# Scores in steps of four PSUM banks with shared diagonal columns, and earlier weight loads, in a planned two-layer attention and feed-forward kernel

## Chip, cores and metric

The kernel runs on one core of one Trainium2 chip. The metric is device time in microseconds (us) of one launch; a run's number is the median of several launches.

## The reference, cut to what matters

Input `x` is 2048 tokens by 512 numbers in bf16. Two kinds of layer alternate, with the same weights each time: attention, feed-forward, attention, feed-forward.

```
x = x + A(layernorm(x)); x = x + B(layernorm(x)); x = x + A(layernorm(x)); x = x + B(layernorm(x))

A: q, k, v = x @ wq, x @ wk, x @ wv           # 32 heads of 16; 4 segments of 512 tokens
   for each segment s:
      p = softmax(q_s k_s^T / 4 + causal mask)          # within the segment
      o_s = g * (phi(q_s) M) / (phi(q_s) z + 1e-6) + (1 - g) * (p v_s)      # g = sigmoid(beta), per head
      M += phi(k_s)^T v_s;  z += sum of phi(k_s)        # phi(t) = t + 1 where t > 0, else exp(t)
   return o @ wo                                         # 512 x 512
B: (gelu(x @ w_gate) * (x @ w_up)) @ w_down             # 512 x 1792, 512 x 1792, 1792 x 512
```

## The kernel before, in words

**Units of work.** There are eight attention blocks `Att(k)`, k = 0 to 7 (four segments, two layers), and eight feed-forward blocks `Ffn(k)`. Everything is kept in SBUF; activations stay transposed (features on partitions). A dense product `product` (L458 to L463) is four matmuls side by side in the four 32-column strips of the array, over 512 moving columns; `dense` strings four or fourteen of them into one PSUM bank, and `evict` (L454 on VectorE, L455 on ScalarE, whichever the plan finds free first) or an addition (L1054, into the residual) empties it.

**Scores.** `steps_of(k)` cuts the causal score blocks of a segment into 20 steps. The heads come in chunks `b` of eight: four groups of 32 partitions, each with an even head in the first 16 rows and an odd one in the last 16 (`par` 0 and 1). A step fills four banks of 512 columns, one per group, with matmuls in the four 32-row strips of the array (L893): for even heads `kf` with 16 rows is the stationary side, for odd heads `kB`, a copy of the keys in which the even rows are zero. `scores` then issues the exp (L924) in two halves of two banks, 128 x 1024 each, into `pt`, and GpSimd masks the diagonal blocks of 128 x 128 (`affine_select`, L911). The score banks `st0` and `st1` (two each) are fixed, and four banks `m0` to `m3` serve all else.

```
sts = {n: psp.tile([P, 2, L], F32, tag=f"st{n}", bufs=1, name="st") for n in halves}
...
if all(free):
    return (0, 1)
other = any(not j[4] and j[0] <= st_free[1] for j in ck.act.jobs)
return (0,) if free[0] and (idle and k >= HALF_FROM or k < HALF_STEPS and not other) else ()
```

So a step may be visited in two halves (`score_now`): the first as soon as its two banks are free, the second later. `flush_item` (L957) multiplies the masked exps with the values `vaug` (four strips of columns again, with the row sum as a 17th value), and VectorE transposes, divides and transposes back (L981 to L996). For `k` in `SPLIT`, which is the last block only, queries go in two halves of 256, so that the feed-forward behind it can start on the first half (`self.parts` = 2).

**The order of work** is a plan made while the kernel is built. `Clocks` and `Engine` model every engine's time with costs written in the code. A loop at the end picks for TensorE, at the modelled time, a score step if its inputs are there and its banks free, else the next operation of the open item, else the ready item with the smallest due time (`DUE`, `DUE_STEP`, `BIAS`). If nothing is ready and scores are still to come, it issues one product on the constant tile `warm` as filler (L1347, printed at L463). Other engines take jobs by ready time plus a slack. The result is a fixed order on each engine; on the chip, semaphores enforce the data's order.

**Loads** go on SP's queue. `x`, key, query and value weights come first (L333 to L340); the others are `pieces` with planned times: third input segment at 14 us, fourth at 27, output projection 32, gate 37, up 49.8, down 94. The same queue issues the DMA transposes of normed rows (`turn_later`, L428), of phi(k) and of the memory's part, and the shift of the odd heads' keys into `kB` (L636).

**The start** is written out by hand (L1183 to L1249): 19 warm-up products (`WARM`, L366), the norms of the first four tiles, transposes on TensorE, the first key and query columns, and one first score step at a planned 9.9 us.

## Time and profile before

| | |
|---|---|
| median of 3 runs | 557.91 us (557.37 to 557.98) |
| profiled execution's span, first to last instruction | 555.8 us |
| TensorE busy | 547.5 us, 99% |
| VectorE / ScalarE / GpSimd busy | 434.5 / 447.8 / 233.3 us |
| exps of scores, L924 | 320 of 128 x 1024, 1026 ns each |
| masks, L911 | 414, 204.4 us |
| filler on `warm`, L463 | 80 matmuls |

The profiled execution's own time outside the profiler is not given apart from its span; the median of the runs lies 2.1 us above the span. PE is TensorE's matmuls, PEld its weight loads, DVE VectorE, ACT ScalarE, POOL GpSimd, SP the queue that issues most DMAs. In a row of a group stand the line, the engine, the operation, out<-in, shapes and count, then the busy time and the mean of one in ns, then the idle time just before and what ended it. In a row of stretches stand the stretch, its length, and the busy time (and instructions) of PE, PEld, DVE, ACT and POOL, then TensorE's granted clock, the DMA share and GB/s.

### The profile page before, as it was taken

The numbers are of one execution on the slowest core, as the hardware profiler recorded it, in microseconds if no ns is written. First come the engines' busy times: TensorE is split into PE (matmuls) and PEld (weight loads), VectorE is DVE, ScalarE is ACT, GpSimd is POOL, SyncE is SP. The second block draws the span as 40 slices with busy tenths as digits, with TensorE's granted clock in tenths as the row PEclk, the third lists the DMA queues.
The fourth block names the chain that finished last, engine by engine and source line by source line (L and its number), as shares of the span: only waits on it lengthen the run. The fifth ranks groups of instructions, "written<-read, shape, count | busy, mean of one in ns | idle before, by whom it ended". The sixth has DMA issues, their size and how long they took to land.

```text
span 555.8 us, 25686 instructions
## 1 busy us (share of the span) xinstructions
PE 547.5 (99%) x11557; PEld 272.5 (49%) x11557; DVE 434.5 (78%) x820; ACT 447.8 (81%) x544; POOL 233.3 (42%) x470
## 2 busy tenths in 40 slices
PE   8999999999999999999999999999999999999997
PEld 4433344444454444444444444544454444545996
DVE  5978797999969898687967889489876898587161
ACT  5899999987998878987898978988889877973500
POOL 5675664255624455144632555155632562021000
PEclk9999999999999999999999999999999999999999
DMA  7248710610152024220230205101320104020001
GB/s 228 40 107 220 150 25 13 168 37 2 22 60 50 12 31 69 40 41 2 41 50 12 42 2 86 33 16 28 79 59 3 22 13 87 3 22 31 14 4 40
DMA packets 65261, 27.87 MB, mean 50 GB/s; under 512 B 54720, under 2 KB 64704, under 8 KB 65152
## 3 DMA queue, kind: packets, MB, share of 16 engines
q1 hardware_dynamic: 65008, 26.23, 23.3%
q8 instruction: 90, 1.47, 1.1%
q14 instruction: 19, 0.16, 0.1%
q10 hardware_dynamic: 144, 0.01, 0.0%
HBM read 9.71 MB, written 2.10 MB: 21 GB/s over the span
## 4 chain that ended last, share of the span: by engine, by line
PE 88%; DVE 6%; DMA 2%; POOL 1%; ACT 1%; issue 1%; SPq 0%; ACTq 0%
PE m L463 71%; PE st L893 9%; PE m L957 6%; DVE xn L522 2%; PE m L366 1%; ACT pt L924 1%; DVE byq L981 1%; DVE x_sb L1054 1%; DMA xnT<-xn 1%; DMA amT<-am 1%; POOL rs L509 1%; POOL pt L911 1%; DVE st L486 0%; DVE ab L989 0%; DVE xnT L454 0%
## 5 line engine op out<-in xcount | busy, mean ns | idle before, releaser
L924 ACT ACTIVATE pt<-st 128x1024 bf16<-128x1024 f32 x320 | 309.8, 1026 | 55.5 <-PE st L893 49.8
L911 POOL TENSOR_SCALAR_AFFINE_SELECT pt<-pt 128x256 bf16<-128x256 bf16 (+2 forms) x414 | 204.4, 510 | 265.5 <-ACT pt L924 249.5
L463 PE MATMUL m<-wd_sb,gel 128*32 128x512 bf16 x1792 | 106.1, 380 | 0.4 <-DVE x_sb L1054 0.4
L463 PE MATMUL m<-xnT,wg_sb 128*32 128x512 bf16 (+1 forms) x2016 | 105.4, 356 | 0.8 <-DVE byq L981 0.5
L463 PE MATMUL m<-xnT,wu_sb 128*32 128x512 bf16 (+1 forms) x2016 | 106.0, 356 | 0.1
L1141 DVE TENSOR_TENSOR gel<-gel,m 128x512 bf16<-128x512 bf16 x112 | 75.3, 682 | 34.3 <-PE m L463 31.6
L463 PEld LDWEIGHTS <-wu_sb 128*32 128x32 bf16 x2016 | 52.3, 97 | 40.0 <-issue 4.8
L463 PEld LDWEIGHTS <-wg_sb 128*32 128x32 bf16 x2016 | 51.7, 97 | 39.7 <-issue 5.9
L463 PEld LDWEIGHTS <-gel 128*32 128x32 bf16 x1792 | 50.6, 97 | 40.3 <-issue 5.0
L1054 DVE TENSOR_TENSOR x_sb<-x_sb,m 128x512 bf16<-128x512 bf16 x64 | 42.2, 671 | 22.5 <-PE m L463 22.4
L981 DVE STREAM_TRANSPOSE byq<-m 128x512 f32<-128x512 f32 x64 | 45.2, 706 | 11.5 <-PE m L957 11.4
L957 PE MATMUL m<-pt,vaug 128*32 128x256 bf16 (+3 forms) x1096 | 46.3, 292 | 0.0
L1106 ACT ACTIVATE gel<-m 128x512 bf16<-128x512 f32 x63 | 34.9, 602 | 11.0 <-PE m L463 11.0
L893 PE MATMUL st<-q,kB 32*128 32x256 bf16 (+3 forms) x548 | 41.0, 290 | 0.0
L486 DVE BATCH_NORM_STATS2 st<-x_sb 128x6 f32<-128x512 bf16 x60 | 40.6, 677 | 0.3
L893 PE MATMUL st<-q,kf 16*128 16x256 bf16 (+3 forms) x548 | 39.1, 293 | 0.5 <-ACT q L1228 0.5
L463 PE MATMUL m<-xnT,wq_sb 128*32 128x512 bf16 (+1 forms) x528 | 36.5, 374 | 0.7 <-DVE xnT L564 0.5
L463 PE MATMUL m<-xnT,wk_sb 128*32 128x512 bf16 (+2 forms) x528 | 35.9, 374 | 0.0
L893 PEld LDWEIGHTS <-kf 16*128 16x128 bf16 x548 | 12.2, 91 | 45.5 <-issue 44.3
L957 PEld LDWEIGHTS <-vaug 128*32 128x32 bf16 x1096 | 24.3, 96 | 20.7 <-issue 7.8
L522 DVE TENSOR_SCALAR xn<-x_sb,mv,rs 128x512 bf16<-128x512 bf16 x64 | 29.9, 512 | 2.8 <-POOL rs L509 2.6
L463 PE MATMUL m<-wv_sb,xnT 128*32 128x512 bf16 x512 | 32.1, 380 | 0.0
(91 smaller groups left out, 539.7 us busy)
## 6 DMA issues: line engine op xcount, KB each, us to landing
out_dram<-x_sb SPq DMA_DIRECT2D x16, 128.0 KB, 2.2
wg_sb<-in_B_w_gate_dram SPq DMA_DIRECT2D x8, 224.0 KB, 3.5
kB<-kf SPq DMA_DIRECT2D x28, 64.0 KB, 2.5
wu_sb<-in_B_w_up_dram SPq DMA_DIRECT2D x8, 224.0 KB, 3.9
wd_sb<-in_B_w_down_dram SPq DMA_DIRECT2D x7, 256.0 KB, 3.1
x_sb<-in_A_x_dram SPq DMA_DIRECT2D x3, 512.0 KB, 6.3
xnT<-xn SPq DMA_TRANSPOSE x48, 3.2
x_sb<-in_A_x_dram SPq DMA_DIRECT2D x4, 128.0 KB, 2.8
```

What stands on the lines that cost most here:

```text
L366: nc.tensor.matmul(ps[:], lhsT=warm[:], rhs=wide, start=True, stop=True)
L463: nc.tensor.matmul(out[r], lhsT=lhsT[:, r], rhs=rhs, start=start, stop=stop, tile_position=(0, 32 * c))
L486: nc.vector.bn_stats(out=self.st6[:, 0, :], in_=x_sb[:, self.tt0 + j, :])
L522: nc.vector.tensor_scalar(out=xn[:], in0=x_sb[:, self.tt0 + j, :], scalar1=self.mv[:, j, 0:1], scalar2=self.rs[:, j, :], op0=ALU.subtract, ...
L893: nc.tensor.matmul(sts[j // 2][:, j % 2, c0:c0 + q1 - q0], lhsT=lhsT[rows, b, P * ki:P * ki + P], rhs=self.q[rows, b, q0:q1], start=True, ...
L911: nc.gpsimd.affine_select(out=dv, in_=dv, pattern=[[0, w], [1, P]], compare_op=ALU.is_ge, fill=0.0, base=0, channel_multiplier=-1)
L924: 1.024, lambda st=st, tile2=tile2: nc.scalar.activation(out=tile2[:], in_=st[:], func=ACT.Exp, scale=SCALE), told), table="exp")
L957: nc.tensor.matmul(ps()[32 * j:32 * j + 32, q0 + shift:q1 + shift], lhsT=self.vaug[:, ki, h * (DH + 1):h * (DH + 1) + 32], rhs=step["pt"][ ...
L981: nc.vector.transpose(out=self.byq[:, c], in_=ps()[:])
L1054: ck.dve.post(ck.made(), slack, (0.683, lambda: nc.vector.tensor_tensor(out=xt, in0=xt, in1=ps()[:], op=ALU.add), lambda t: (ps.read(t), t ...
L1106: return lambda: nc.scalar.activation(out=out(), in_=in_(), func=ACT.Gelu_apprx_tanh)
L1141: ck.dve.post(ck.made(), NORMAL, (0.683, lambda: nc.vector.tensor_tensor(out=hidden(g, h), in0=hidden(g, h), in1=banked(ps), op=ALU.mult), ...
```

## The change

It does the following.

1. *Shared diagonal columns.* In a diagonal block of 128 queries, the first 64 queries see only 64 keys. `kS` holds the first 64 keys of every tile for an even and an odd head, interleaved, and one block of 64 columns gives the scores of both (`u` = 2 in the code below). Matching values `vS` are made by two DMAs per block. The other 64 queries keep their 128 keys. Steps become 18 in a segment, 19 in the first.
2. *Steps of four banks.* All eight banks are one pool. A step takes four banks, side by side if they are free, and then has one exp of 128 x 2048; otherwise two pairs. Half visits are gone. `may_open` limits how many banks other items hold.
3. *First segment by halves*: `SPLIT = {0, NK - 1}`.
4. *Port and landings in the plan*: the model of VectorE and GpSimd has jobs marked `Port` that exclude each other, and items of the first feed-forward block wait in the plan until their weights are modelled as landed.
5. *Loads*: output projection and gate from 8.8 us, third input segment 9.3, up 26, down 43.1 (three pieces) and 47 (four), fourth input segment 59.6.
6. Two sets of values and of `kB` in place of three, the masks of the memory's block in bf16, the gate folded into the division; a shorter hand-written start with 14 warm-up products; the last down product in 384 and 128 columns; and new numbers for the plan, with a table `CHANGES` that alters slacks and due times every 8 us of planned time.

The core of the diff:

```diff
-WARM = 19
-STEPS = 20
+WARM = 14
+WG_GAP, WU_GAP, WD2 = 1.1751, 1.964, 47.0
-WO, WG, X2, WU, X3, WD = 32.0, 37.0, 14.0, 49.8, 27.0, 94.0
+WO, WG, X2, WU, X3, WD = 8.92, 8.8357, 9.3414, 26.0, 59.6, 43.1
-SPLIT = {NK - 1}
+SPLIT = {0, NK - 1}
...
+    def shared(blocks, tiles):
+        return [(b, 2, t, P * t, P * t + Q, Q * (len(blocks) * m + n)) for n, b in enumerate(blocks)
+                for m, t in enumerate(tiles)]
...
+    def long(b, par):
+        return [(b, par, 3, L - Q, L, 0), (b, par, 0, Q, L, Q)], []
+    def short(b, par, ends):
+        return [(b, par, 1, P + Q, L, 0), (b, par, 2, HALF + Q, L, 320)], ends
...
+        found += [long(b, 0), short(b, 0, []), (shared((b, b + 1), range(TPS)), [(b, 0, None)]),
+                  long(b, 1), short(b, 1, [(b, 1, None)])]
+        for par in range(2):
+            found += [long(b + 1, par), short(b + 1, par, [(b + 1, par, None)])]
...
+            if isinstance(cost, Port):
+                t = next((end for who, begun, end in self.port[-24:] if who is not self and begun <= t < end), t)
+                self.port.append((self, t, t + cost))
...
     for h in range(7):
-        pieces.append((WD + 2.0 * h, 256, lambda r=r: load(
+        pieces.append(("down", (WD if h < 3 else WD2) + 0.1 * h, 256, lambda r=r: load(
...
+    big = psp.tile([P, 8, L], F32, tag="big", bufs=1, name="big")
...
+            def shared_keys(blocks, t):
+                def copy(b, u, eng):
+                    eng.tensor_scalar(
+                        out=kS[:, b, :, :, u], in0=self.kf[:, b, :].rearrange("p (t h c) -> p t h c", h=2, c=Q)[:, :, 0, :],
+                        scalar1=(maskA, maskB)[u][:, 0:1], scalar2=None, op0=ALU.mult)
+                ...
+                    for u in range(2):
+                        ck.pool.post(t, tn.KS_SLACK + 0.01 * b, (Port(1.05), lambda b=b, u=u: copy(b, u, nc.gpsimd), (
+                            lambda t2, b=b: ev.update({("kS", k, b): t2})) if u else None))
...
+    def may_open():
+        return held("m") < (tn.CAP if step_ready() else tn.CAP_FREE) and len(free_banks()) > 0
...
+    def four_banks():
+        free = free_banks()
+        for first in (4, 0, 3, 2, 1):
+            if WHOLE and all(first + i in free for i in range(4)):
+                return [first + i for i in range(4)]
+        ...
+        return [*pairs[1], *pairs[0]] if len(pairs) > 1 else None
...
+        for b, u, ki, q0, q1, c0 in parts:
+            for j in range(4):
+                rows = slice(32 * j, 32 * j + (32 if u else 16))
+                if u == 2:
+                    lhsT = kS[rows, b, ki].rearrange("p c u -> p (c u)")
+                else:
+                    lhsT = (a.kf, a.kB)[u][rows, b, P * ki:P * ki + P]
+                nc.tensor.matmul(big[:, got[j], c0:c0 + q1 - q0], lhsT=lhsT, rhs=a.q[rows, b, q0:q1], start=True,
+                                 stop=True, tile_position=(32 * j, 0))
...
+            ck.act.post(max(ready, step["at"]), tn.EXP_SLACK, (
+                0.172 + 0.000832 * width * len(banks_of), lambda g=g, st=st: nc.scalar.activation(
+                    out=pt[:, g, 0:width], in_=st, func=ACT.Exp, scale=SCALE), lambda t, g=g: told(t, g, g is groups[-1])),
+                table="exp")
...
+                return [down(j, slice(0, 3 * P)), down(j, slice(3 * P, D))]
...
+    def timely():
+        last = max((f for f, o in zip(banks, owner) if o == "s"), default=0.0)
+        return last <= ck.pe + tn.AHEAD or tn.EAGER and not opened and not any(it.ready() for it in items if it.kind != "flush")
```

In a flush, `pieces` holds, for a head, the plain blocks with `vaug` and the shared blocks with `vS`, eight in a whole flush instead of four, over the same 1280 columns. After, the plan still issues filler on `warm` where nothing is ready.

869 lines of the change are left out of this document (530 added, 339 removed).

## The prediction

> **What bounds the kernel now.** I read the page's busy table and its chain first, then the cores' clock, the busy time by stretches, the groups, the waits, and last the timeline of TensorE.
>
> ```profile
> span 555.8 us, 25686 instructions
> PE 547.5 (99%) x11557; PEld 272.5 (49%) x11557; DVE 434.5 (78%) x820; ACT 447.8 (81%) x544; POOL 233.3 (42%) x470
> PE 88%; DVE 6%; DMA 2%; POOL 1%; ACT 1%; issue 1%; SPq 0%; ACTq 0%
> core 0: 555.8 us, clock 0.999
> 40.00:60.00 20.00, 20.00 (x346) 8.05 (x340) 17.32 (x36) 19.73 (x27) 11.65 (x26) 1.00 0.81 194
> 60.00:80.00 20.00, 19.56 (x372) 8.08 (x372) 16.69 (x35) 19.47 (x24) 12.77 (x27) 1.00 0.44 93
> 300.00:320.00 20.00, 20.00 (x440) 9.24 (x436) 18.27 (x35) 17.50 (x21) 9.87 (x21) 1.00 0.19 36
> 520.00:540.00 20.00, 19.87 (x744) 19.51 (x736) 9.57 (x14) 5.86 (x10) 0.00 (x0) 1.00 0.02 4
> ```
>
> TensorE (PE) is busy in 19.6 to 20.0 of every 20 us in these stretches, and 88% of the chain is its own. It runs at full clock, so only less work on PE, or work on it that was worth nothing, can shorten the kernel. Up to 80 us ScalarE (ACT) is full too (19.5 to 19.7 of 20); at 300 it is not (17.5), and at 520 it has little left to do. So the early stage has two limits, the rest has one.
>
> What PE's time is made of shows in its timeline, the columns being start, length, engine and line, operation, count:
>
> ```profile
> 305.93 1.04 PE L463 MATMUL m<-xnT,wk_sb 128*32 128x512 bf16 x16
> 306.90 0.39 PE L893 MATMUL st<-q,kB 32*128 32x512 bf16 x4
> 307.22 2.56 PE L463 MATMUL m<-xnT,wu_sb 128*32 128x512 bf16 x44
> 511.58 3.20 PE L463 MATMUL m<-wd_sb,gel 128*32 128x512 bf16 x56
> 514.60 6.29 PE L463 MATMUL m<-xnT,wg_sb 128*32 128x256 bf16 x224
> ```
>
> Fourteen dense products of four matmuls take from 511.58 to 514.60, 0.216 us each. At 305.93 four of them should be done by 306.79, but the score matmuls of L893 begin at 306.90: 0.11 us to go from the column tiling of the dense work to the row tiling of the scores. From 306.90 to the next dense matmul at 307.22 are 0.32 us, of which 0.21 are the 512 columns and 0.11 the way back. A visit of PE to the scores costs 0.43 us, half of it for switching the tiling.
>
> ```profile
> 10.11 0.29 PE L893 MATMUL st<-q,kf 16*128 16x256 bf16 x4 [0.49 <-ACT q L1228]
> 499.88 0.29 PE L893 MATMUL st<-q,kf 16*128 16x256 bf16 x4
> PEld L893 <- issue: 71.5, 173, 0.5
> 25.28 1.48 PE L463 MATMUL m<-warm 128*32 128x512 bf16 x24
> 75.69 0.39 PE L463 MATMUL m<-warm 128*32 128x512 bf16 x4
> L463 PE MATMUL m<-warm 128*32 128x512 bf16 x80 | 5.8, 382 | 0.0
> ```
>
> The timeline has 181 separate visits, the first at 10.11 and the last at 499.88 (the weight loads of L893 waited 173 times for their turn, which is the same count less the visits that waited for data). There are only 160 steps of scores; the others are steps done in two halves, each paying the full 0.43 us. And 80 matmuls on the constant tile `warm`, that is 20 products or 4.3 us, are filler that the planner put in where nothing was ready, between 25.28 and 77 us, in the stage where ACT is full.
>
> **The change part by part.** *Four-bank steps and shared diagonals.* A segment has 20 steps before. After, the first 64 queries of each diagonal block see only 64 keys, and the keys of two heads are interleaved into one block, so the diff's `steps_of` gives 18 steps for segments 1 to 7 and 19 for segment 0: 145. Each is one visit, never half. Removed are 181 - 145 = 36 visits at 0.43 us: **-15.5 us** of PE.
>
> *Smaller pieces.* Fifteen of the 145 steps have eight parts of 64 columns in place of one or two long ones, and a flush (L957) takes four more products of 64 columns, 64 times, for the same 1280 columns. The trace has no 64-column matmul; its neighbours are these.
>
> ```profile
> 464.62 0.23 PE L893 MATMUL st<-q,kf 16*128 16x128 bf16 x4
> 464.68 0.23 PE L893 MATMUL st<-q,kB 32*128 32x128 bf16 x4
> 464.96 1.70 PE L463 MATMUL m<-wd_sb,gel 128*32 128x512 bf16 x28
> 312.97 0.64 PE L463 MATMUL m<-zcols,phiq 128*32 128x8 bf16 x64
> 313.44 1.06 PE L463 MATMUL m<-wv_sb,xnT 128*32 128x512 bf16 x16
> ```
>
> A score part of 128 columns starts 0.06 us after the one before, and the visit with four of them still ends after 0.34 us (464.62 to 464.96). Sixteen products of 8 columns took 0.47 us (312.97 to 313.44), 0.029 each, which leaves 64 columns (0.027 us of streaming) hardly dearer than streaming. If 64 columns cost as little as 0.029, a step of eight parts grows by 0.02 us and a flush by 0.01: 15 x 0.02 + 64 x 0.01 = 0.9 us. If they cost 0.06 as 128 do, it is 15 x (8 x 0.06 - 0.21) + 64 x 4 x (0.06 - 0.027) = 4.1 + 8.4 = 12.5 us. They cannot be cheaper than the columns they stream. I take **+1.5 us**, near the row of 8 columns, since the distance between 128-column parts is their streaming (0.053).
>
> *One exp over four banks.*
>
> ```profile
> L924 ACT ACTIVATE pt<-st 128x1024 bf16<-128x1024 f32 x320 | 309.8, 1026 | 55.5 <-PE st L893 49.8 <-POOL pt L911 4.6
> L455 ACT ACTIVATE q<-m 128x512 bf16<-128x512 f32 x17 | 10.3, 604 | 0.8 <-PE m L463 0.5
> 60.33 7.65 ACT L924 ACTIVATE pt<-st 128x1024 bf16<-128x1024 f32 x8
> ```
>
> From 512 to 1024 columns ACT takes 0.42 us more, so 2048 should take 1.026 + 2 x 0.42 = 1.87 us. Before, a pair takes 1.94 (309.8 / 160; the eight at 60.33 take 7.65, the same). ACT's exps go from 309.8 to 145 x 1.87 = 271, or to 281 if every step is still issued as two pairs. This is off the chain after 100 us and worth nothing there by itself. In the early stage it is what the filler waited for: at 60.33 ACT runs exps without a gap while PE runs filler. With segment 0 cut into two halves (so that its first output projection and gate products become ready after 6 steps instead of 20) and the weights loaded from 8.8 us on, I count the filler as gone: **-4.3 us** (0 at worst).
>
> *VectorE and GpSimd.* The masks shrink: a step before has up to eight blocks of 128 wide columns to mask, after it two narrow ones over half the partitions. In their place come 56 copies of keys on GpSimd (POOL) at 1.05 us by the planner's own figure, 59 us.
>
> ```profile
> L911 POOL TENSOR_SCALAR_AFFINE_SELECT pt<-pt 128x256 bf16<-128x256 bf16 x332 | 146.8, 460 | 188.5 <-ACT pt L924 173.1 <-PE m L463 9.9
> L911 POOL TENSOR_SCALAR_AFFINE_SELECT pt<-pt 128x512 bf16<-128x512 bf16 x74 | 49.4, 670 | 72.5 <-ACT pt L924 72.0
> L911 POOL TENSOR_SCALAR_AFFINE_SELECT pt<-pt 128x1024 bf16<-128x1024 bf16 x8 | 8.6, 1094 | 4.4 <-ACT pt L924 4.4
> 13.12 1.80 POOL L418 MEMSET kB<- 128x2048 bf16 x1
> 13.27 1.77 DVE L644 TENSOR_SCALAR kB<-kf,maskB 128x384 bf16<-128x384 bf16 x1
> L644 DVE TENSOR_SCALAR kB<-kf,maskB 128x512 bf16<-128x512 bf16 x3 | 1.1, 387 | 0.0
> ```
>
> An unsplit segment has 16 plain steps with two masks of 256 elements (0.46 each) and two shared ones with two of 1024 (1.09): 19 us, about 155 us over all segments against 205 before. With the copies POOL stays near 235 us. But POOL holds up VectorE (DVE): the copy at 13.27 took 1.77 us beside POOL's memset, where larger ones take 0.387. DVE has 121 us without work, so I put this at 0 on PE; what it costs if it strikes an eviction that PE waits for is a rival below. [...]
>
> *Loads.*
>
> ```profile
> wg_sb<-in_B_w_gate_dram SPq DMA_DIRECT2D x8, 224.0 KB, 3.5
> wd_sb<-in_B_w_down_dram SPq DMA_DIRECT2D x7, 256.0 KB, 3.1
> ```
>
> The output projection, the gate weights and the third segment's input (512 + 8 x 224 + 512 KB, 2.8 MB) are issued from 8.8 us, the up weights from 26, the down weights at 43 to 47 instead of 94. On SP's queue the transposes of the normed rows, the key shifts and the phi transposes come behind them. Between 40 and 60 us the kernel already moves 194 GB/s with PE at 20.00 of 20, so I cost this at 0; without that cover, 1.8 MB of down weights at that rate are 9 us that a transpose issued behind them could be late, and PE would run filler: at most 9 us.
>
> *Ends.* Warm-up falls from 19 to 14 matmuls and the first scores come some 1.6 us sooner by the planner, but the dense start stays at 11.4: 0. The last down product is cut into 384 and 128 columns:
>
> ```profile
> 552.26 0.69 DVE L1054 TENSOR_TENSOR x_sb<-x_sb,m 128x512 bf16<-128x512 bf16 x1 [2.33 <-PE m L463]
> ```
>
> The last addition, 0.69 us for 512 columns, is then about 0.29 for 128: **-0.4 us**.
>
> **The sum**: 555.8 - 15.5 + 1.5 - 4.3 - 0.4 = 537.1 us of span. The median before is 557.91, 2.1 us above the profiled span, which I add: **539.2, said as 539**.
>
> **The rivals.**
>
> *A, the early stage stays bound by ACT.* For it: 60 us to 80 has ACT at 19.47. Of the 181 visits 59 lie before 80 us by the same count; if those and the filler give nothing, the gain is 15.5 x 122/181 = 10.4, and the time 557.9 - 10.4 + 1.5 - 0.4 = 548.6. Against it: ACT's own work per segment falls by 10 to 12%.
>
> *B, slower: PE stands at the visits.* Before, the first pair of banks is free after 1.03 us of exp and a visit may begin with it; after, all four stay taken for 1.87, and the visit with everything dense behind it in PE's order waits for the last of them.
>
> ```profile
> ACT pt L924 <- PE st L893: 49.8, 80, 1.8
> PE st L893 <- ACT q L1228: 0.5, 1, 0.5
> ```
>
> The gain of the sum is 15.5 + 4.3 + 0.4 - 1.5 = 18.7 us. To make the kernel slower by more than 1.1 us (0.2%), the waits must reach 19.8 us, 0.14 us at each of 145 visits; 0.25 us at each would give 539.2 + 36 = 575. For it: the order on PE is fixed by a planner's figures, and the hand-over between exps and scores is slow already (ACT waited 49.8 us in 80 gaps for scores). Against it: PE waits for ACT once, 0.5 us, in all of before, and dense work may now use the other four banks and more.
>
> *C, POOL's copies hold up DVE where PE needs a bank.* If one in three of the 56 copies puts 0.5 us on PE, that is +9: 548. [...]
>
> ```profile
> PE m L463 <- DVE byq L981: 0.8, 3, 0.5
> ```
>
> *D, better: the start tightens too.* PE's own small waits (some 3 us in all, that row the largest after the first microsecond) and the 1.6 us by which the first scores come sooner are won as well, with 1.5 for the small pieces not paid: 539.2 - 3 - 1.6 - 1.5 = 533.
>
> **How the numbers follow.** The forecast has 0.50, A 0.15, C 0.08, D 0.12, B 0.12; 0.03 is left for a change within 0.2% (1.1 us), about what a measurement of this kernel can tell from none. The range goes from just below D, 531, to the forecast with the dear end of the small pieces (539.2 + 11 = 550.2) and A, with a little over it: 553. Faster has 0.85, the same 0.03, slower 0.12.
>
> **What would show it.** Right, if the profile after has about 145 visits of 0.43 us (0.34 to 0.5 where there are eight parts), exps of 1.87 us over 2048 columns, fewer than 20 products of `warm`, PE at 99% and steps of 64 columns at 0.03 us a part. Wrong, if PE's idle time names ACT's exp or a DVE eviction for more than a few us, if filler between 10 and 80 us grows, if the shared steps take over 0.6 us, or if a load stands in front of a transpose that PE waits for.

## The result and the profile after

The changed kernel takes 557.8 us (median of 10 runs, 556.5 to 560.3); the kernel before, on the same chip, 558.0 (10 runs, 557.4 to 558.9). The ratio is 0.9999, 95% interval 0.9985 to 1.0013: no change, where 539 (531 to 553) had been forecast. The profiled execution has a span of 554.7 us, 1.1 less than before; it is the fastest of the ten (556.5 us), and four of the others ran at a mean clock of 0.994 to 0.997, so what is read from it below leaves the last 1.3 us up to the median open.

From the page of the changed kernel, the span, TensorE's busy time and the chain; then its page's row for instruction transfers, of which the kernel before had 90 with 1.47 MB:

```profile
span 554.7 us, 29909 instructions
...
PE 540.0 (97%) x13722; PEld 293.8 (53%) x13722; DVE 432.6 (78%) x830; ACT 419.6 (76%) x386; POOL 237.9 (43%) x416
...
q8 instruction: 107, 1.75, 1.3%
...
PE 80%; DVE 9%; DMA 4%; ACT 3%; issue 2%; POOL 1%; SPq 0%; ACTq 0%; DVEq 0%; POOLq 0%
```

PE is busy 7.5 us less, but no longer 99% of the span, and 20% of the chain is other things where it was 12%. There are 4,223 more instructions. PE alone has more than these: 2,165 more matmuls, each with its weight load. The waits of PE in the changed kernel (us in total, times, longest):

```profile
PE big L654 <- issue: 2.9, 4, 1.5
PE big L1117 <- issue: 1.9, 1, 1.9
PE big L654 <- DMA xnT<-xn: 1.7, 3, 0.8
PE big L1117 <- DMA vS<-vaug: 1.2, 1, 1.2
...
PE big L1421 <- ACT pt L1491: 0.5, 2, 0.3
```

4.8 us of them are "issue": nothing that the profile shows was missing. The timeline of PE at these places, and at one with filler:

```profile
58.98 0.38 PE L1117 MATMUL big<-pt,vaug 128*32 128x256 bf16 x8
61.23 0.21 PE L1117 MATMUL big<-pt,vaug 128*32 128x64 bf16 x4 [1.88 <-issue]
...
93.50 1.69 PE L654 MATMUL big<-warm 128*32 128x512 bf16 x28
95.58 1.05 PE L654 MATMUL big<-xnT,wq_sb 128*32 128x512 bf16 x16 [0.38 <-DMA xnT<-xn]
...
116.06 0.41 PE L1421 MATMUL big<-q,kS 32*128 32x64 bf16 x32
116.40 0.51 PE L654 MATMUL big<-xnT,wu_sb 128*32 128x256 bf16 x12
116.74 0.62 PE L654 MATMUL big<-zcols,phiq 128*32 128x8 bf16 x56
118.87 0.21 PE L654 MATMUL big<-zcols,phiq 128*32 128x8 bf16 x8 [1.51 <-issue]
```

PE stops in the middle of a flush (L1117) and in the middle of 64 small matmuls (`zcols`) for which the profile shows no operand missing. At 93.50 it runs seven products of filler and then still waits for the next segment's rows.

I summed the timeline of PE from each start to the next, with gaps over 0.12 us apart:

| us of PE | before | after | change |
|---|---|---|---|
| score visits (181, 145) | 59.3 | 48.1 | -11.2 |
| dense work, with the switch into each visit | 420.8 | 416.7 | -4.1 |
| flushes | 35.9 | 38.1 | +2.2 |
| filler (20, 49 products) | 5.2 | 12.1 | +6.9 |
| gaps | 3.3 | 10.4 | +7.1 |
| warm-up | 6.8 | 5.2 | -1.6 |

With +0.2 in the small products and -0.6 at the end that is the 1.1 us. So the visits gave what they should, and filler and gaps took 14.0 us back. Two windows of the same 30 us, before and then after, show where (busy us and count of PE, PEld, DVE, ACT, POOL, then clock, DMA share, GB/s):

```profile
45.00:75.00 30.00, 30.00 (x524) 12.08 (x524) 26.46 (x56) 29.24 (x38) 17.39 (x38) 1.00 0.68 152
```
```profile
45.00:75.00 30.00, 25.99 (x960) 20.68 (x952) 23.67 (x49) 24.67 (x27) 11.30 (x16) 1.00 0.55 119
```

After, PE got 960 matmuls where it had 524, and was busy 4 us less.

### The profile page after: what moved, and what is told of

Same layout as the page of the kernel before. It is cut to its first block, busy times and chain, and to the rows that moved or that the text cites. A ratio compares the mean times of both kernels' runs of the same rounds, so it can differ in the third digit from the quotient of the medians.

```text
span 554.7 us, 29909 instructions
## 1 busy us (share of the span) xinstructions
PE 540.0 (97%) x13722; PEld 293.8 (53%) x13722; DVE 432.6 (78%) x830; ACT 419.6 (76%) x386; POOL 237.9 (43%) x416
## 3 DMA queue, kind: packets, MB, share of 16 engines
q8 instruction: 107, 1.75, 1.3%
## 4 chain that ended last, share of the span: by engine, by line
PE 80%; DVE 9%; DMA 4%; ACT 3%; issue 2%; POOL 1%; SPq 0%; ACTq 0%; DVEq 0%; POOLq 0%
PE big L654 68%; PE big L1421 7%; PE big L1117 5%; ACT pt L1491 3%; DMA amT<-am 1%; DVE xn L713 1%; DVE byq L1145 1%; DVE st L677 1%; DMA xnT<-xn 1%; DVE ab L1153 1%; POOL pt L1464 1%; DMA vS<-vaug 1%; DMA x_sb<-in_A_x_dram 1%; DVE x_sb L1218 1%; DVE aT L1160 1%
## 5 line engine op out<-in xcount | busy, mean ns | idle before, releaser
L1491 ACT ACTIVATE pt<-big 128x2048 bf16<-128x2048 f32 (+1 forms) x151 | 272.8, 1810 | 68.8 <-PE big L1421 63.7
L1464 POOL TENSOR_SCALAR_AFFINE_SELECT pt<-pt 64x256 bf16<-64x256 bf16 (+4 forms) x302 | 151.9, 530 | 232.7 <-ACT pt L1491 231.4
L654 PE MATMUL big<-xnT,wu_sb 128*32 128x512 bf16 (+1 forms) x2240 | 105.6, 337 | 0.9 <-issue 0.9
L654 PE MATMUL big<-wd_sb,gel 128*32 128x512 bf16 (+2 forms) x1848 | 105.2, 373 | 0.0
L654 PE MATMUL big<-xnT,wg_sb 128*32 128x512 bf16 (+1 forms) x2240 | 104.7, 337 | 0.0
L1308 DVE TENSOR_TENSOR gel<-gel,big 128x512 bf16<-128x512 bf16 x112 | 75.0, 682 | 32.0 <-PE big L654 26.9
L654 PEld LDWEIGHTS <-gel 128*32 128x32 bf16 x1848 | 46.6, 97 | 43.3 <-issue 3.6
L1218 DVE TENSOR_TENSOR x_sb<-x_sb,big 128x512 bf16<-128x512 bf16 (+1 forms) x65 | 43.1, 668 | 25.6 <-PE big L654 25.3
L1145 DVE STREAM_TRANSPOSE byq<-big 128x512 f32<-128x512 f32 x64 | 45.2, 706 | 20.5 <-PE big L1117 20.0
L1117 PE MATMUL big<-pt,vaug 128*32 128x64 bf16 (+5 forms) x1152 | 45.0, 263 | 2.1 <-issue 1.9
L1273 ACT ACTIVATE gel<-big 128x512 bf16<-128x512 f32 x64 | 35.2, 605 | 4.5 <-PE big L654 4.3
L1117 PE MATMUL big<-pt,vS 128*32 128x64 bf16 x960 | 28.0, 193 | 1.2 <-DMA vS<-vaug 1.2
```

Source lines behind the costliest of these rows:

```text
L654: nc.tensor.matmul(out[r], lhsT=lhsT[:, r], rhs=rhs, start=start, stop=stop, tile_position=(0, 32 * c))
L1117: nc.tensor.matmul(ps()[32 * j:32 * j + 32, q0 + shift:q1 + shift], lhsT=va[:, ki, values_of(va, b, p, j)], rhs=step["pt"][:, j, c0:c0 + q ...
L1145: nc.vector.transpose(out=self.byq[:, c], in_=ps()[:])
L1218: ck.dve.post(ck.made(), slack, (0.683 - 0.00104 * (D - width), lambda: nc.vector.tensor_tensor(out=xt, in0=xt, in1=ps()[:, 0:width], op=A ...
L1273: return lambda: nc.scalar.activation(out=out(), in_=in_(), func=ACT.Gelu_apprx_tanh)
L1308: ck.dve.post(ck.made(), NORMAL, (0.683, lambda: nc.vector.tensor_tensor(out=hidden(g, h), in0=hidden(g, h), in1=banked(ps), op=ALU.mult), ...
```

## Experiments on the filler

My first theory after the result: the filler stands where PE would wait anyway, so a shorter step on PE only makes more of it. The rival is the prediction's: filler is work on PE's path, and goes when it goes.

**a_nofill**: the changed kernel without its 44 planned filler products (five more are written into its start and stay); **b_nofill**: the kernel before without its 20.

```
-                product(ps()[:], warm[:], wide)
+                ck.tiling("columns")
```

> The changed kernel with the plan as it is, but the 44 filler products on the constant tile (9.5 us of TensorE) that the plan puts in are not issued. Theory 'cover': they stand where TensorE would wait for data anyhow, mostly for VectorE in the first 45 us and around 133 us; the time falls by 0 to 2 us and idle time of the same size appears in their place. Rival 'plan too slow': the data is there earlier than the plan thinks, the filler is in the way, and the time falls by 7 to 9.5 us, to about 549.

> The kernel before without the 20 filler products that its plan puts between 25.3 and 77 us (5.2 us of TensorE by the trace); the order of everything else is unchanged. Theory 'filler stands where TensorE would wait anyway, and keeps its granted clock up': the time doesn't fall; it stays or rises by up to 4 us (557.5 to 562), and the profile shows gaps of 1 to 2.5 us at 25 to 29 us and near 63 and 76 us, with a granted clock below 1 right behind them. Rival, the prediction's own term 'filler is work on TensorE's path that goes when it goes': 5.2 us less, near 552.8.

a_nofill took 564.2 us, 1.0113 (1.0095 to 1.0132) of the kernel before; b_nofill 559.7, 1.0040 (1.0027 to 1.0053). Both are slower. For b_nofill that is what its theory said; neither forecast for a_nofill came, since its idle time appeared but the time rose by 6.4 us. Waits, timeline and windows of a_nofill:

```profile
PE big L654 <- DMA xnT<-xn: 6.2, 2, 3.5
PE big L1421 <- ACT pt L1491: 5.6, 7, 1.9
...
25.98 0.29 PE L1421 MATMUL big<-q,kf 16*128 16x128 bf16 x4 [1.93 <-ACT pt L1491]
28.63 0.40 PE L1421 MATMUL big<-q,kf 16*128 16x256 bf16 x4 [1.27 <-ACT pt L1491]
100.75 1.00 PE L654 MATMUL big<-xnT,wq_sb 128*32 128x512 bf16 x8 [3.49 <-DMA xnT<-xn]
...
25.00:30.00 5.00, 2.75 (x48) 1.28 (x51) 4.72 (x13) 3.97 (x4) 2.45 (x3) 0.57 0.74 139
30.00:35.00 5.00, 5.00 (x84) 2.16 (x80) 3.58 (x10) 3.77 (x4) 4.21 (x6) 0.74 0.43 127
100.00:105.00 5.00, 4.25 (x96) 2.08 (x100) 1.20 (x4) 1.25 (x2) 0.33 (x1) 0.66 0.31 61
```

Where the filler of 22 to 29 us was, PE now waits for the exp to give back its banks; where the filler of 93 us was, for `xnT`. Gaps rise from 10.4 to 19.4 us and all but eat the 10.3 us of filler that went. On top the granted clock (third number from the end) falls: it is 0.50 from 25.75 to 32.57 us, from 49.64 to 53.05 and from 100.84 to 104.25, of which the stretches of 5 us show parts as 0.57 to 0.74. Its mean is 0.987, and 1.3% of 562 us is 7 us. By the same sums as in the table PE's other work takes 8.0 us longer and the end 1.0: 9.0 + 8.0 + 1.0 - 10.3 makes the 7.7 us between the spans. b_nofill closes in the same way: 5.2 us of filler gone, gaps up by 2.9, and a mean clock of 0.993 (3.9 us): +1.6, the difference of the spans (557.4 against 555.8). So filler covers waits, and without it the clock fell: a mean of 0.987 in a_nofill's profile against 1.000 in the changed kernel's, 0.993 in b_nofill's against 0.999 before.

**b_nohalf**: why are there more such waits after? The kernel before, but with its steps always on all four banks (no visit of two banks while the exp of the other two runs), the order worked out anew.

```
-HALF_FROM = 0
+HALF_FROM = NK
-HALF_STEPS = 1
+HALF_STEPS = 0
```

> The kernel before with its steps always on all four banks: no visit of two banks while the exp of the other two runs. The order is worked out anew with constants that were fitted to the other one, so its later part may be worse for that reason; what is to be read is the first 45 us, up to which the order follows the exps. Theory 'a step that takes four banks at once makes exp and visit take turns, so ACT is not kept busy in the start and TensorE waits or is filled': exps of the first 45 us no longer follow each other without a gap, ACT's busy time there falls by 2 us or more, filler there rises from 2.5 us (25 to 29 us) to 4 us or more; the whole is 5 to 20 us slower. Rival 'the start is paced by VectorE and the inputs, the steps' shape doesn't matter there': ACT's exps and the filler up to 45 us are as before within 0.5 us.

575.1 us, 1.0305 (1.0283 to 1.0326), with 25.6 us of filler. As its constants belong to another order, only the start is read. ACT's timeline there: before, then b_nohalf, then the changed kernel.

```profile
25.47 7.56 ACT L924 ACTIVATE pt<-st 128x1024 bf16<-128x1024 f32 x8 [1.75 <-PE st L893]
```
```profile
27.49 1.94 ACT L924 ACTIVATE pt<-st 128x1024 bf16<-128x1024 f32 x2 [2.96 <-PE st L893]
30.01 1.94 ACT L924 ACTIVATE pt<-st 128x1024 bf16<-128x1024 f32 x2
33.01 1.94 ACT L924 ACTIVATE pt<-st 128x1024 bf16<-128x1024 f32 x2
```
```profile
24.03 1.89 ACT L1491 ACTIVATE pt<-big 128x2048 bf16<-128x2048 f32 x1
26.89 1.88 ACT L1491 ACTIVATE pt<-big 128x2048 bf16<-128x2048 f32 x1 [0.97 <-PE big L1421]
29.39 1.88 ACT L1491 ACTIVATE pt<-big 128x2048 bf16<-128x2048 f32 x1
```

Before, the exps of two banks follow each other without a break, four steps in 7.56 us, because a visit fills one pair while ACT empties the other. On four banks at once a step comes every 2.5 to 3.0 us, in b_nohalf as in the changed kernel. ACT's busy time up to 45 us falls from 36.1 to 34.0 us (32.6 in the changed kernel), filler up to 45 us rises from 11 products to 24 (25 planned ones, and 5 in the start, in the changed kernel). The theory's numbers hold. The start is paced by exps, as the prediction saw, but it became slower in steps per microsecond although ACT had less to do: between 25 and 45 us the exps of 9 steps end before, of 6.5 in b_nohalf, of 7 in the changed kernel.

Up to 20 us, however, the exps of 3.5, 3 and 1 steps have ended. So four banks at once don't explain the changed kernel's first 20 us: there its order runs the query and key products from 11.61 to 17.9 us without a visit, where the kernel before has visits at 12.77, 13.64, 15.38 and 17.77, and ACT's second step begins at 18.67. No run tests this alone.

## Experiments that take rivals away

**a_noks**: without the 56 copies of keys on GpSimd, so later segments' diagonal columns use old keys (rival C). **a_wd60**: down weights sent for at 60 and 64 us; **b_wd61**: in the kernel before, at 62.6, the second part of the change alone. **a_2exp**: each exp of four banks as two of two.

```
-                        ck.pool.post(t, tn.KS_SLACK + 0.01 * b, (Port(1.05), lambda b=b, u=u: copy(b, u, nc.gpsimd), (
+                        ck.pool.post(t, tn.KS_SLACK + 0.01 * b, (Port(1.05), lambda b=b, u=u: None, (
...
-WG_GAP, WU_GAP, WD2 = 1.1751, 1.964, 47.0
+WG_GAP, WU_GAP, WD2 = 1.1751, 1.964, 64.0
-WO, WG, X2, WU, X3, WD = 8.92, 8.8357, 9.3414, 26.0, 59.6, 43.1
+WO, WG, X2, WU, X3, WD = 8.92, 8.8357, 9.3414, 26.0, 59.6, 60.0
...
-WO, WG, X2, WU, X3, WD = 32.0, 37.0, 14.0, 49.8, 27.0, 94.0
+WO, WG, X2, WU, X3, WD = 32.0, 37.0, 14.0, 49.8, 27.0, 62.6
...
-                    out=pt[:, g, 0:width], in_=st, func=ACT.Exp, scale=SCALE), ...
+                    out=pt[:, slice(g.start + h, g.start + h + 2), 0:width], in_=st[:, h:h + 2, :], func=ACT.Exp, scale=SCALE)
+                    for h in range(0, g.stop - g.start, 2)], ...
```

> The changed kernel without the 56 copies of keys on GpSimd (segments 1 to 7 score their shared columns against old keys; 58 us of GpSimd work left out). Theory 'port': these copies hold up VectorE where TensorE needs it; VectorE's busy time falls by 5 us or more and the time by 3 to 9 us. Rival 'off the path': the time falls by less than 1 us.

> The changed kernel with the down weights issued at 60 and 64 us of the plan instead of 43.1 and 47. The order on all engines but SP's queue stays the same. Theory 'loads': the down weights right behind the up weights hold up transposes, key shifts or the instruction stream between 43 and 72 us; then the idle time of TensorE at 46 and between 59 and 72 us (4 us) goes, and the time falls by 2 to 4 us. Rival 'not the loads': the idle time stays and the time is the same within 0.7 us.

> One part of the change alone: the kernel before, with its down weights sent for at 62.6 us instead of 94 (right behind the up weights), the order of all engines but SP's the same. Theory 'where the down weights load costs and gains nothing': 0.998 to 1.002 of the kernel before. Rival 'earlier down weights delay the segment inputs behind them (the third and later xn loads), so TensorE waits for xnT': 1 to 3 us slower, with a DMA wait near 70 to 100 us.

> The changed kernel, with each exp over four banks issued as two over two banks (1024 columns each), in the same place of the same order: 139 more ACT instructions, nothing else. In the trace of the kernel before an exp of 1024 columns took 0.94 us, in that of the changed one one of 2048 took 1.88 us, so ACT gains or loses nothing by the sums (2 x 0.94). Theory 'ACT's time is not what limits the changed kernel; TensorE's own waits are': no change, 0.998 to 1.004 of the changed kernel. Rival 'the long exp holds the four banks as one and so the first matmuls of the next visit wait the whole 1.88 us': the visit still needs all four banks in the order it writes them, so the first half would be free 0.94 us sooner; in the first 60 us, where exps follow each other every 2.6 to 2.9 us, up to 0.3 us for each of some 15 steps would come back, 3 to 5 us, ratio 0.991 to 0.995.

| run | us | ratio to before | interval |
|---|---|---|---|
| a_noks | 557.9 | 1.0003 | 0.9982 to 1.0024 |
| a_wd60 | 559.0 | 1.0023 | 1.0002 to 1.0044 |
| b_wd61 | 557.6 | 1.0001 | 0.9987 to 1.0015 |
| a_2exp | 556.9 | 0.9986 | 0.9969 to 1.0003 |

None of them is what took the gain. In a_noks VectorE is busy 428.3 us instead of 432.6, so the copies do cost it 4 us (less than the 5 expected), but PE's issue gaps stay (waits of a_noks):

```profile
PE big L654 <- issue: 2.5, 3, 1.4
PE big L1117 <- issue: 2.1, 1, 2.1
```

Loading the down weights right behind the up weights neither helps nor hurts. Sent for later, in a_wd60, the kernel took 1.2 us more than the changed kernel, which is neither of its two forecasts; the intervals of the two overlap, so it isn't known whether this is a cost. The earlier loads of the output projection, the gate and up weights and the inputs were not tested alone. One exp or two for a step makes no difference that these runs can tell.

## Experiments on the issue gaps

Theory: PE runs out of instructions where many short ones lie together. Rival: the places themselves (banks, tiling) are to blame.

**a_thin**: gate and up of the first segment issue two of their four strips, so half of these hidden units keep old data. **b_cut**: the kernel before with gate and up of its first two segments cut into products of 256 columns. (By the trace these are 896 matmuls that became 1,792, half of the numbers in the expectation.)

```
-        for c in range(4):
+        for c in range(strips):          # 2 for gate and up of k = 0
...
+                if k < 2:                # b_cut: two products of 256 columns for one of 512
+                    return [(Clocks.MM[512], lambda kt=kt, f=f: cut(kt, f)) for f in tiles(g) for kt in range(KT)]
```

> The changed kernel in which the gate and up products of the first feed-forward block, which are cut into 256 columns there, issue two of their four column strips (the other half of those hidden units keeps old data). Each product streams the same 256 columns, so TensorE's streaming time is the same, but 896 matmuls with their weight loads fewer pass through its instruction stream. Theory 'instruction supply': the idle time put down to issue (4.8 us at 59, 64, 68, 71 and 117 us) goes or shrinks to under 2 us, and the time falls by 2 to 5 us. Rival 'loads' or any other: that idle time stays over 4 us and the time is the same within 1 us.

> The kernel before with gate and up products of the first two segments cut into two of 256 columns each: 1,792 products of 512 columns become 3,584 of 256, the same columns and flops, the same order of all else. Theory 'instructions reach TensorE's queue at a limited rate, and where many short ones lie together it runs dry': the profile of this kernel shows gaps of TensorE put down to issue of 1 to 3 us in the first 150 us, which the kernel before lacks there, more KB of instruction transfers, and more time than the added 1,792 products cost by themselves. A product of 128 columns takes 0.056 us and one of 512 0.216 us in the trace, so halving costs no more than 0.005 us each, about 0 to 9 us; the gaps would come on top. Rival 'the gaps put down to issue come from the changed order's full banks or from its visits of many small pieces': no issue gap over 0.5 us here, and the time rises by 9 us at most.

a_thin: 554.9 us, 0.9958 (0.9942 to 0.9974), with 448 matmuls fewer and the same columns streamed; its issue gaps are 0.3 us in all, from 4.8. b_cut: 561.7 us, 1.0074 (1.0053 to 1.0094); its waits name one issue gap of 0.8 us at 108 us, where the kernel before has none, less than the 1 to 3 us expected. The theory passes the first run clearly and the second barely: most of b_cut's 4 us lies in the halved products themselves.

**c_whole**: the same work in fewer instructions. Gate of the first segment's first half, up of its second half and the `zcols` products of segment 2 go out as one matmul over the whole array instead of four strips: 384 fewer (a half has 56 products, not the 64 of the expectation). **c_again** is the same kernel measured once more. **c_both** adds the exps in halves. **d_whole** does so with all gate and up products of the first segment, two memory updates and the `zcols` of segment 1 as well, 864 fewer by the trace (its expectation and the later ones say 816).

```
+    def at_once(out, lhsT, rhs, start=True, stop=True):
+        ck.tiling("columns")
+        nc.tensor.matmul(out, lhsT=lhsT, rhs=rhs, start=start, stop=stop)
...
-                         lambda kt=kt, f=f, n=n: product(ps()...
+                         lambda kt=kt, f=f, n=n: (at_once if whole else product)(ps()...
```

> The changed kernel, order and filler as they are, with three stretches of products issued as one matmul of 128x128 weights each instead of four of 128x32 side by side: gate of the first segment's first half, up of its second half (64 products of 256 columns each) and the normaliser products of segment 2 (16 of 8 columns): 144 instructions where there were 576. Nothing is left out. A product takes as long as before by its columns (0.107 us for 256), and going over to whole weights and back is dearer by two switches of about 0.1 us for each of two stretches. Theory 'the issue gaps are TensorE running out of instructions, since the changed kernel has many short ones in these stretches': the gaps put down to issue at 59.4 (1.88 us) and 117.4 (1.51 us) go or shrink below 0.3 us, those at 64 to 71 (1.4 us together) shrink in part; the kernel gains 2 to 4 us, ratio to the kernel before 0.992 to 0.997. Rival 'the gaps belong to these places whatever is issued there': they stay, and the time is unchanged or 0.5 us longer.

> The kernel of the run before in this list and the exps in two halves of two banks each together. The exps in halves alone measured 0.9986 (0.9969 to 1.0003) of the kernel before, the changed kernel 0.9999: if the two add, 0.991 to 0.996. If the exps' halves do nothing, the same as the run before within 0.1%.

> The kernel with gate of the first half, up of the second half and the normaliser products of segment 2 as whole 128x128 matmuls, carried further: all gate and up products of the first segment, both memory updates of segments 0 and 1 and the normaliser products of segments 1 and 2 as whole matmuls, 816 fewer instructions than in the changed kernel in place of 384. Nothing is left out, the order and the filler are unchanged. In the profile of the run with 384 fewer, 1.1 us of issue gaps were left, nearly all at the normaliser products of segment 1 near 66 us (0.89 and 0.18). Theory 'every gap put down to issue is missing instructions': these go too; against that stand some three more switches of about 0.1 us; 0.5 to 1.2 us less than the run with 384 fewer, ratio to the kernel before 0.990 to 0.993. Rival 'the first stretches had all that there was to gain': no less than that run, 0.992 to 0.996.

| run | us | ratio to before | interval | issue gaps, waits for xnT (us) |
|---|---|---|---|---|
| changed kernel | 557.8 | 0.9999 | 0.9985 to 1.0013 | 4.8, 1.7 |
| c_whole | 553.2 | 0.9925 | 0.9908 to 0.9943 | 1.1, 1.6 |
| c_again | 553.2 | 0.9937 | 0.9913 to 0.9961 | 1.3, 2.7 |
| c_both | 554.9 | 0.9952 | 0.9934 to 0.9970 | 0.6, 5.8 |
| d_whole | 557.4 | 0.9986 | 0.9965 to 1.0006 | none, 7.8 |

The place of the second gap in c_whole's timeline, now without one:

```profile
114.41 0.50 PE L658 MATMUL big<-xnT,wu_sb 128*128 128x256 bf16 x3
114.75 0.55 PE L658 MATMUL big<-zcols,phiq 128*128 128x8 bf16 x16
115.22 1.05 PE L654 MATMUL big<-xnT,wk_sb 128*32 128x512 bf16 x16
```

So the gaps are missing instructions: with nothing left out and the same order, they go where the count falls (from 4.8 us to 1.1), and c_whole is faster than both kernels. The traces bear it out directly, since they hold the time of each transfer of instructions, a block of 16.4 KB (1.75 MB over 107). All twenty profiles together have 39 gaps of PE that are put down to issue, and each of them ends 1.2 to 1.6 us after such a block has landed. In the changed kernel there are five, 1.3 to 1.5 us behind: the one that ends at 61.23 us follows the block of 58.33 to 59.82, the one that ends at 118.87 follows that of 116.28 to 117.57. The 13,722 matmuls over 107 blocks are 128 a block on the mean, each with its weight load. In none of the profiles do two blocks begin less than 3.3 us apart (3.41 at least in the changed kernel, 3.47 before), and 128 matmuls of 256 columns take 3.6 us (212 take 5.93). Shorter ones use a block up sooner than that: in the flush from 58.42 us 44 take 0.94 us, which makes 2.7 for 128, and of `zcols` 56 take 0.62 from 116.74, which makes 1.4.

c_both adds nothing: it is 1.7 us slower than c_whole, with 5.8 us of waits for `xnT`, which is neither of its forecasts. And d_whole, which has no issue gap left, gains nothing in time: my expectation for it failed. Another wait had come up in their place.

## Experiments on the landing of the next segment

The waits of PE in d_whole, its timeline at 49 us, and what SP's queue issues before the second such wait:

```profile
PE big L654 <- DMA xnT<-xn: 7.8, 4, 2.7
...
49.39 1.05 PE L654 MATMUL big<-xnT,wq_sb 128*32 128x512 bf16 x16 [2.73 <-DMA xnT<-xn]
...
88.76 1.40 SPq L892 DMA_DIRECT2D vS<-vaug  x2
90.25 2.57 SPq L611 DMA_TRANSPOSE amT<-am  x2
92.91 2.39 SPq L611 DMA_TRANSPOSE xnT<-xn  x1
```

The change adds two transfers per segment, `vS<-vaug`, which put the values into the order of the shared diagonal blocks. They stand in SP's queue ahead of the last transposition of the next segment's rows, for which PE waits until 96.6 us.

**d_novs**: d_whole without these copies from the second segment on, so the later diagonal columns use the first segment's values. **d_vspool**: the copies issued on GpSimd's queue. **d_wu**: the up weights' pieces sent for 1.2 us apart instead of 1.96. **a_vspool** and **c_vspool**: the changed kernel and c_whole with the copies on GpSimd's queue.

```
-            ck.sp.post(t, tn.KB_SLACK, (0.55, lambda u=u, c=c: nc.sync.dma_start(
+            ck.sp.post(t, tn.KB_SLACK, (0.55, lambda u=u, c=c: nc.gpsimd.dma_start(
                            out=vS[u:P:2, :, c], in_=self.vaug[0:Q, :, c]), ...
```

> A second time the kernel with 384 fewer instructions (gate of the first half, up of the second half, normaliser of segment 2 as whole matmuls), beside the three that follow. Its first measurement was 553.18 us, 0.9925 (0.9908 to 0.9943), the kernel with 816 fewer 0.9986 (0.9965 to 1.0006) with 7.8 us of waits for xnT in its profile where this one had 1.6. Theory 'when the issue gaps are gone, the time hangs on the landing of the next segments' xnT, which differs from run to run': its times spread over 551 to 560 like those of the other, mean ratio 0.992 to 0.998. Rival 'this one is steadily faster': 0.991 to 0.9945 again.

> The kernel with 816 fewer instructions without the copies of shared values (vS) from the second segment on: 14 of the 16 transfers of 136 KB left out, so the later segments' diagonal columns use the first segment's values. The order of everything else is unchanged. Theory 'the new vS transfers, which SP issues just ahead of the next segment's last xnT transposition, delay its landing': the waits for xnT near 94 and 147 us (2.55 and 2.16 us) go or shrink below 0.8; the one at 46.7 us (2.7 us), which has no vS transfer just before it, stays; the time falls by 3 to 6 us, clock losses behind the gaps included, to 0.988 to 0.993 of the kernel before. Rival 'the transpositions themselves are late, whatever stands beside them': all three waits stay, the time within 0.2% of 0.9986.

> The kernel with 816 fewer instructions with the vS copies issued on GpSimd's queue in place of SP's: nothing is left out. In the trace SP is held 0.7 us by each of the two and 1.2 to 1.3 by each transposition behind them, one after the other. Theory 'what delays xnT is SP's queue': xnT starts 1.4 us sooner and the waits at 94 and 147 us shrink by about 1.4 us each, ratio 0.992 to 0.997. Rival 'what delays xnT is the transfers' share of the DMA engines': the waits stay as they were, 0.997 to 1.002; GpSimd's own work, held up by the issues, may add a wait for masked scores.

> The kernel with 816 fewer instructions with the up weights' eight pieces sent for 1.2 us apart instead of 1.96, from 26 us on as before: they are through before the transpositions near 44 us instead of lying around them. The order on TensorE, VectorE, ScalarE and GpSimd is unchanged. Theory 'the wait for xnT at 46.7 us (2.7 us in one profile, 0.3 to 0.8 in others) comes from the weights' pieces around it': it shrinks below 0.5 us, the granted clock behind it stays up, 1 to 3 us less, ratio 0.993 to 0.997. Rival 'the down weights or the copies of kB beside it do it': it stays, 0.997 to 1.001.

> The changed kernel with nothing but the vS copies issued on GpSimd's queue in place of SP's. Theory 'two causes, instructions and vS on SP's queue, each worth some 3 to 5 us': 0.990 to 0.996 of the kernel before, and the issue gaps (4.8 us in the changed kernel's profile) stay. Rival 'moving vS helps only where the issue gaps are gone, since otherwise TensorE reaches the boundary later than xnT anyway': 0.997 to 1.001.

> Both remedies in the smaller form: 384 fewer instructions (gate of the first half, up of the second, normaliser of segment 2) and the vS copies on GpSimd's queue. With 816 fewer and vS on GpSimd's queue 0.9915 (0.9884 to 0.9946) was measured, with 384 fewer alone 0.9925 and 0.9937. If the two causes add: 0.987 to 0.992, below both kernels, 550 to 553 us; the profile shows 1.1 to 1.3 us of issue gaps near 63 to 67 us and no wait for vS at 144 us. If the landing's own scatter decides: 0.992 to 0.996.

| run | us | ratio to before | interval | issue gaps, waits for xnT (us) |
|---|---|---|---|---|
| d_novs | 549.9 | 0.9867 | 0.9851 to 0.9882 | none, 1.7 |
| d_vspool | 552.0 | 0.9915 | 0.9884 to 0.9946 | 0.2, 3.7 |
| d_wu | 556.9 | 0.9991 | 0.9969 to 1.0013 | none, 4.4 |
| a_vspool | 556.2 | 0.9991 | 0.9971 to 1.0011 | 3.5, 1.7 |
| c_vspool | 553.3 | 0.9926 | 0.9900 to 0.9953 | 1.2, 1.3 |

c_again repeats c_whole (552.0 to 556.3 us), so that kernel is steadily faster, as the rival to its theory had it.

Without the copies d_whole falls by 7.4 us, more than the 3 to 6 expected. Its windows at the third boundary, d_whole first and then d_novs:

```profile
145.00:150.00 5.00, 2.84 (x76) 1.25 (x68) 4.86 (x12) 2.77 (x3) 2.46 (x5) 0.97 0.71 88
150.00:155.00 5.00, 5.00 (x72) 1.85 (x68) 1.01 (x3) 3.34 (x4) 1.87 (x4) 0.69 0.01 2
149.72:153.13 3.41, 3.41 (x38) 1.13 (x41) 0.52 (x1) 2.37 (x2) 2.04 (x4) 0.50 0.01 2
```
```profile
145.00:150.00 5.00, 5.00 (x116) 2.19 (x112) 4.93 (x10) 4.76 (x7) 3.94 (x6) 1.00 0.02 5
150.00:155.00 5.00, 4.47 (x171) 2.62 (x156) 4.90 (x9) 4.91 (x6) 1.72 (x5) 1.00 0.01 3
```

In d_whole PE is idle for 2.2 of the first five microseconds and then has half its clock from 149.72 to 153.13 us, which is the 0.69 of the next five; in d_novs neither happens. At the second boundary the wait falls from 2.55 to 1.38 us, less than expected. But the wait near 46.7 us, which was expected to stay, falls from 2.73 us to 0.33:

```profile
47.05 1.05 PE L654 MATMUL big<-xnT,wq_sb 128*32 128x512 bf16 x16 [0.33 <-DMA xnT<-xn]
```

The copies nearest ahead of it stand at 27 us, and both kernels have them. So 2.4 of the 7.4 us are not shown to come from the copies.

Moving the copies to another queue, with nothing left out, brings 5.4 us (d_vspool), just past the expected range. On SP's queue `amT` now follows the transposition before it after 1.4 us (85.84 to 87.25) where it took 2.8 (87.43 to 90.25), and `xnT` after 4.4 us (to 90.26) where it took 5.5 (to 92.91). The 1.4 us that were expected at each boundary came at the third (the wait falls from 2.16 to 0.77 us) but not at the second (2.55 to 2.06), and here too the wait near 46.7 us fell, to 0.90. SP's queue in d_whole, the row ahead of those shown, and then in d_vspool:

```profile
87.43 1.22 SPq L611 DMA_TRANSPOSE phik<-e  x1
```
```profile
85.84 1.32 SPq L611 DMA_TRANSPOSE phik<-e  x1
87.25 2.91 SPq L611 DMA_TRANSPOSE amT<-am  x2
90.26 2.08 SPq L611 DMA_TRANSPOSE xnT<-xn  x1
```

The two remedies don't add in all forms: on the changed kernel itself and on c_whole, which wait little for `xnT`, moving the copies shows no gain (a_vspool, c_vspool), as the rival to a_vspool had it. d_wu failed: the wait at 46.6 us stayed (3.0 us, now put down to a down weight's transfer beside it). Left open is why the transposition before that boundary lands 2.5 us after its issue in one kernel and over 4 us in another with the same order (2.4 to 3.0 us in c_whole's four, 3.0 to 4.3 in d_whole's), and so how much of the difference between c_whole and d_whole, and of the gain of d_novs and d_vspool over d_whole, would be there again in another layout of the program.

## Why the prediction was wrong, by its own steps

- **Visits, -15.5: right.** 145 visits; -11.2 in the visits and -4.1 in the dense rows that hold the switch into them, -15.3.
- **Smaller pieces, +1.5: nearly right.** A visit of eight parts takes 0.34 us (116.06 to 116.40), one of two 0.33 (97.11 to 97.44); the flushes cost +2.2. The dear end of 12.5 was far off as a cost of streaming. What these pieces cost as instructions was not priced at all.
- **One exp of 1.87: right**, 1.879 us:

```profile
L1491 ACT ACTIVATE pt<-big 128x2048 bf16<-128x2048 f32 x139 | 261.1, 1879 | 60.3 <-PE big L1421 55.3 <-POOL pt L1464 3.7
```

- **Filler gone, -4.3: wrong, +6.9. This is the step that failed first.** It asked whether ACT had less to do, not how often it would get a step. With two-bank halves, exp and visit overlapped; with four banks as one they take turns, and ACT waits for scores in a stage that it paces (b_nohalf, a_nofill). That ACT was full up to 80 us was read from rows that begin at 40; up to 45 us it was busy for 36.1. The 20 products take 5.2 us by the timeline, not 4.3, and the bound "0 at worst" had no reason behind it. Of the 29 products more, 14 are planned ones up to 45 us, and b_nohalf alone brings 13 there. Five stand in the start, and ten come later, seven of them in the wait for `xnT` at 93 us; no run shows why the start and the other late ones need theirs.
- **Loads, 0: right for the down weights, wrong for the queue.** Sent for at 43, 60, 62.6 or 94 us they give the same time within 0.25%. But "on SP's queue the transposes come behind them" should have been said of the `vS` copies, which the diff adds to each segment and which were not counted: 2.9 us of waits for `vS` and `xnT` in the changed kernel, at most 5 of the 7.4 us of time in d_whole. Taken out of SP's queue in the changed kernel itself they bring nothing that the runs can tell from none (a_vspool).
- **Gaps of PE, not in the sum: wrong, +7.1**, 4.8 of it instructions that were not there in time (a_thin, c_whole, and the blocks' landings).
- **Ends, -0.4: right**; the last addition, of 128 columns, takes 0.29 us.
- **POOL's copies, 0: right** (a_noks); POOL has 237.9 us, 235 was said. Rival C is out.
- **Rival A** named the right stage and the wrong price: the stage does not merely keep its old length, it grows. **Rival B** named the right mechanism, PE standing before banks that wait for the exp. In the changed kernel's profile it looks refuted (0.5 us of waits for ACT), because filler lies over it; without the filler it is 5.6 us. **D** did not come: the 1.6 us went out of the warm-up, but five products of filler (1.8 us) stand in the start instead, and the first scores begin 0.5 us sooner (9.57 against 10.11), not 1.6. The total came out within 0.1% of the kernel before, which the prediction gave a chance of 0.03: visits that were won and filler and gaps that were added cancel by chance, not by a mechanism.

## What to carry to other kernels

Filler can be a wait in disguise, as it was here (a_nofill: 10.3 us of it out, the time 6.4 us up): before counting it as gain, take it out and read what the engine then waits for. When a change merges steps, count the hand-overs between two engines as well as their work: here two half buffers that alternate ended the exps of 9 steps between 25 and 45 us, one whole buffer those of 7, though its exp takes 1.88 us against 1.94 for the two halves. And give every added transfer and every added instruction a place in its queue: here the waits for instructions and for transfers took back some 7 of the 15.3 us that 36 fewer visits had won, and filler another 6.9.

## What the runs showed of the hardware

- **TensorE ran dry of instructions.** The changed kernel's transfers of instructions are 107 of 16.4 KB (1.75 MB), one for 128 of its 13,722 matmuls with their weight loads on the mean; the kernel before has 90 for 11,557, again one for 128. Behind two stretches of 212 matmuls of 256 columns without a break (52.49 to 58.42 us and 110.04 to 116.06) PE stood for 1.88 and 1.51 us in the middle of ready work; with 384 matmuls fewer these two gaps were gone (c_whole). Every such gap of the twenty profiles ends 1.2 to 1.6 us after a block's landing. The changed kernel's five came to 4.8 us.
- **The granted clock fell to 0.50 for 3.41 us at a time.** There is one such fall in d_whole (from 149.72 us), and in a_nofill two in a row (from 25.75) and one each from 49.64 and 100.84. The waits there lasted 2.16 us in d_whole, 1.93 at the first place in a_nofill and 3.49 at the last; behind one of 2.73 us in d_whole, which ended at 49.39, the clock stayed at 1.00. What decides stays open. In the 3.41 us ahead of its fall at 149.72 us d_whole's PE was busy for 1.25; from 47.32 to 50.73, around the end of the wait of 2.73 us, it was busy for 1.34 and the clock stayed at 1.00; in b_nofill it was busy for 2.09 from 64.99 to 68.40, and the clock fell. By an estimate from these numbers a fall costs up to 1.7 us more than the wait, half of 3.41, where PE has work throughout.
- **A whole 128x128 matmul and four strips of 32 took the same time here**: 53 gate products of 256 columns took 6.02 us whole in c_again (52.10 to 58.12) and 5.88 in c_vspool (52.11 to 57.99), and 5.93 us in strips in the changed kernel (52.49 to 58.42). Between these two forms, in this place, only the count of instructions made a difference.
